# Idle-time matmuls of zeros, new decoding costs and new ranks in a list-scheduled attention and mixer kernel

## The chip, the cores and the metric

The kernel runs on one core of a Trainium2 chip. The metric is the device time of one execution in microseconds (us). Three executions of the kernel before took 624.26, 625.16 and 625.78 us; the median is 625.16 us.

## The reference

For 4 batches of 768 positions, 8 heads of width 64 do attention in which a query sees the 8 global positions and the 96 positions up to and including its own, with a bias that falls with distance. The heads side by side give x (768 x 512 per batch), and two mixers follow:

```
scores = q @ k.T / 8 + bias                       # masked; 8 heads of width 64
x  = softmax(scores) @ v                          # heads side by side: [B, 768, 512]
h  = relu(x.T @ w_tok1) @ w_tok2                  # token mixer, 768 -> 256 -> 768
u  = x + h.T
out = u + relu(u @ w_ch1) @ w_ch2                 # channel mixer, 512 -> 1536 -> 512
```

The mixers' weights arrive as 64-bit floats and are decoded on the chip.

## The kernel before

**Work items.** Nothing is issued in the order of the loops. `run` enters every step into a plan with `add(name, engine, cost, run, after, rank, take, give, form)`: the engine (or a choice of engines, each with its cost), a duration in us, the steps that it comes after, a rank (lower goes first), and the rooms and PSUM banks that it takes and gives back. `Plan.record` walks through time by these durations: whenever an engine is free in the plan, it takes the ready step with the lowest rank for which rooms and banks are free. A step for TensorE whose `form` is another than that of the step before costs 0.1 us more, 0.2 us where one of the two forms is None, and `TURN` times this is added to its rank. Banks are taken from the front of a list of free ones and come back at its end. Then the steps are issued in the order found, and `InOrder` pins it: on the chip each engine runs its steps strictly in the plan's order and waits for their data there. The plan starts VectorE at 1.9, ScalarE at 1.4, GpSimd at 3.6, the queue of transfers at 2.6 us (`BUSY`) and TensorE at 0. Each engine's result is taken to be seen by another after 0.11 to 0.2 us, and a transfer's after 1.5 us (`LATENCY`).

**Attention.** A pair `v` (0 to 47, 12 per batch) is two heads by 256 queries: `load`, `q` (scaled queries), `S` (scores on TensorE, tile sp), `max` (VectorE), `exp` (ScalarE), `sum` and `inv`, `norm` (GpSimd), `T` (transposes, tile tp) and `back`, `V` (tile op), `put` (ScalarE copies op into x). From pair 20 on the transposes are made by transfers (`split`, `turn`, `join`). In the plan a pair's `q` has rank r - 8, its `max` r - 10, `sum` and `inv` r - 12, `T` r - 5, `back` and `V` r - 10, `put` r - 15 and the rest r, with r from `rank("pair", v)`: 10 v in batch 0, `120 + 8.5 i` in batch 1.

**Weights.** Thirty pieces `n` of 128 x 512 go through `load`, `down` (ScalarE, t<-w), `shift` (VectorE TENSOR_SCALAR t<-t), `upper` and `lower` (VectorE SCALAR_TENSOR_TENSOR t<-w,t, both), `high` (ScalarE CAST wc<-t) and `low` (wc<-t,wc, on VectorE or GpSimd). Pieces 0 to 5 are the token mixer's, and from piece 6 on two pieces make one of the 12 slices of the channel mixer's weights. Their rank is `40 + 12 n` below 6 and `100 + 12 n` from 6 on (172 to 448); `high` and `low` go 20 lower.

**Mixers.** Each batch has its tokens (`N`/`xtp`, `J`/`pj`, `U`/`pu`, ranks from -20 in batch 0), and then 24 channel steps k, two passes over the 12 slices: `F` (hp, 12 matmuls), ScalarE's hh, VectorE's hl, and `G` (acc, 12 matmuls over four banks held for a whole pass). `F` of slice f comes after `low` of piece 6 + 2f, `G` after that of 7 + 2f. The rank of batch 0's channel steps is `150 + 5 k`, less 6 for `F` and 30 for hh and hl. At the end of a pass VectorE adds the sums (o<-acc,uh and o<-o,ul) into a tile o, which a transfer stores; the next use of that tile waits for the transfer.

Two matmuls of zeros at the start (`warm`) stand ahead of all.

Of the kernel before, what the change touches and what calls it, by code (L numbers as in the profile page):

```python
# [13 lines left out]
BF16 = mybir.dt.bfloat16  # L14
# [10 lines left out]
P = 128  # L25
# [8 lines left out]
RING = 4  # L34
FAR = 20
NEAR = 2
WARM = 2
PER = H // 2 * NU
PIECES = 6 + 2 * NF
# [6 lines left out]
def f32(ap):  # L46
    return ap.bitcast(F32)
# [40 lines left out]
class Plan:  # L88
# [13 lines left out]
    def add(self, name, engine, cost, run, after=(), rank=0.0, take=(), give=(), form=None):  # L102

        costs = engine if isinstance(engine, dict) else {engine: cost}
        self.work[name] = dict(name=name, costs=costs, run=run, after=sorted(set(after)), rank=rank, take=take, give=give,
                               form=form, choice=isinstance(engine, dict))
# [98 lines left out]
class Fast:  # L207
# [42 lines left out]
    def turn(self, out, in_):  # L250
        self.pe.transpose(out, in_, self.ident)


    def setup(self):

        const, early, dve = self.const, self.early, self.dve
        wp = self.ps.tile([P, 512], F32, tag="b7", name="warm")
        for i in range(WARM):
            self.pe.matmul(out=wp, lhsT=early.warm[:, :P], rhs=early.warm, start=i == 0, stop=i == WARM - 1)
        rel, far, glob = early.rel, early.far, early.glob  # L260
        self.scale(0, dve)
        n = self.soft.tile([P, 4], F32, tag="st", name="n")
        dve.tensor_copy(out=n, in_=early.ni)
        ng, nl = n[:, 0:1], n[:, 2:3]
        nl8 = self.soft.tile([P, 1], F32, tag="st", name="nl8")
        dve.tensor_scalar(out=nl8, in0=nl, scalar1=-8.0, scalar2=None, op0=ALU.mult)

        dve.tensor_scalar(out=glob, in0=glob, scalar1=ng, scalar2=-BIG, op0=ALU.is_ge, op1=ALU.mult)


        self.bo, self.bt, self.be = [const.tile([P, w], F32, tag=t, name=t) for t, w in (("bo", 256), ("bt", P), ("be", 256))]
        bo, be = self.bo, self.be
        dve.tensor_scalar(out=rel, in0=rel, scalar1=nl, scalar2=-BIG, op0=ALU.is_ge, op1=ALU.mult)
        dve.tensor_tensor(out=bo[:, 32:], in0=rel, in1=far, op=ALU.add)
        dve.scalar_tensor_tensor(out=self.bt, in0=glob, scalar=nl8, in1=bo[:, 128:], op0=ALU.add, op1=ALU.max)
        dve.tensor_scalar(out=bo[:, :32], in0=glob[:, :32], scalar1=nl8, scalar2=None, op0=ALU.add)
        for o, i, w in ((0, 32, 128), (160, 160, 96), (128, 0, 32)):
            self.pool.tensor_scalar(out=be[:, o:o + w], in0=bo[:, i:i + w], scalar1=1.0, scalar2=0.0, op0=ALU.mult, op1=ALU.add)


    def weights(self, n):

        add, dve, act = self.plan.add, self.dve, self.act
        g = {}

        def load():  # L290
            x, i = self.pieces[n]
            g["w"] = self.wt.tile([P, 512], I64, tag="w", name="w64")
            self.sp.dma_start(out=g["w"], in_=x[:, i:i + 512])

        def words():
            wi = g["w"].bitcast(I32).rearrange("p (n two) -> p n two", two=2)
            return wi[:, :, 0], wi[:, :, 1]

        def down():
            g["t"] = self.io.tile([P, 512], I32, tag="io", name="t32")  # L300
            act.activation(out=f32(g["t"]), in_=f32(words()[1]), func=AF.Copy, scale=DOWN)

        def shift():
            dve.tensor_scalar(out=g["t"], in0=g["t"], scalar1=3, scalar2=None, op0=ALU.logical_shift_left)

        def upper():
            dve.scalar_tensor_tensor(out=g["t"], in0=words()[1], scalar=-0x80000000, in1=g["t"], op0=ALU.bitwise_and,
                                     op1=ALU.bitwise_or)

        def lower():  # L310
            dve.scalar_tensor_tensor(out=g["t"], in0=words()[0], scalar=29, in1=g["t"], op0=ALU.logical_shift_right,
                                     op1=ALU.bitwise_or)

        def high():
            if n < 6:
                dst, i = (self.W1, self.W2)[n // 3], 512 * (n % 3)
                g["h"], g["l"] = dst[0][:, i:i + 512], dst[1][:, i:i + 512]
            else:
                t = self.wt.tile([P, 1024], F32R, tag="w", name="wc")
                g["h"], g["l"] = t[:, :512], t[:, 512:]  # L320
                (self.A, self.Z)[n % 2][n // 2 - 3] = g["h"], g["l"]
            act.copy(out=g["h"], in_=f32(g["t"]))

        def low(engine):
            engine.tensor_tensor(out=g["l"], in0=f32(g["t"]), in1=f32(g["h"]), op=ALU.subtract)

        r = rank("weights", n)
        add(f"w{n}", "sp", 1.85, load, [f"w{n - 1}"] if n else [], rank("load weights", n), ["w", "raw"])
        add(f"down{n}", "act", 0.6, down, [f"w{n}"], r, ["t"])
        add(f"shift{n}", "dve", 0.45, shift, [f"down{n}"], r)  # L330
        add(f"upper{n}", "dve", 0.75, upper, [f"shift{n}"], r)
        add(f"lower{n}", "dve", 0.85, lower, [f"upper{n}"], r, (), ["w", "raw"])
        add(f"high{n}", "act", 0.52, high, [f"lower{n}"], r - 20, ["w"] if n >= 6 else [])
        add(f"low{n}", dict(dve=0.64, pool=1.35), 0, low, [f"high{n}"], r - 20, (), ["t"])


    def load(self, v):
# [179 lines left out]
    def tokens(self, b):  # L517
# [31 lines left out]
        def high(s):  # L549
            rows[s] = tiles()  # L550
            act.copy(out=rows[s][0], in_=g["tp", s])

        def low(s, engine):
            engine.tensor_tensor(out=rows[s][1], in0=g["tp", s], in1=f32(rows[s][0]), op=ALU.subtract)

        def join(s):
            if s == 0:
                g["pj"] = [self.bank("pj", b, j) for j in range(2)]
            x = rows.pop(s)
            for j in range(2):  # L560
                for n, (w, i) in enumerate(((0, 0), (1, 0), (0, 1))):
                    self.pe.matmul(out=g["pj"][j], lhsT=self.W1[w][:, TOK * s + P * j:TOK * s + P * j + P],
                                   rhs=x[i], start=s == 0 and n == 0, stop=s == NS - 1 and n == 2)
# [35 lines left out]
        for s in range(NS):  # L599
            m, i = divmod(s, 3)  # L600
            if b < NEAR:

# [3 lines left out]
            else:  # L606
                for c in range(4 if i == 0 else 0):
# [5 lines left out]
                    [f"xt{b}{m}{c}" for c in range(4)] + ([f"nl{b}{s - 1}"] if s else []), r[s] - 20, ["p"], ["nat"])  # L613
            add(f"nh{b}{s}", "act", 0.5, lambda s=s: high(s), [f"xw{b}{s}" if b >= NEAR else f"N{b}{s}"], r[s] - 15, [tag, tag])
            add(f"nl{b}{s}", dict(dve=0.62, pool=1.4) if b >= NEAR else dict(dve=0.62), 0, lambda en, s=s: low(s, en),
                [f"nh{b}{s}"], r[s] - 15, (), ["p"] if b >= NEAR else [("xtp", b, s)])
            add(f"J{b}{s}", "pe", 1.39, lambda s=s: join(s), [f"nl{b}{s}", f"low{s // 2}"] + ([f"J{b}{s - 1}"] if s else []),
# [93 lines left out]
    def run(self):  # L711
        self.setup()
        for n in range(PIECES):
            self.weights(n)
        for b in range(B):
            for v in range(PER * b, PER * b + PER):
                self.pair(v)
            self.tokens(b)
            self.channel(b)
        self.plan.record()  # L720


# [13 lines left out]
def rank(kind, *at):  # L736

    if kind == "weights":
        return 40.0 + 12.0 * at[0] if at[0] < 6 else 100 + 12 * at[0]
    if kind == "load weights":  # L740
        n = at[0]
        return 8 + 3 * n if n < 8 else 30 + 4 * n
    if kind == "load":
        return 2.5 * at[0]
    if kind == "pair":
        v = at[0]
        b, i = divmod(v, PER)
        if b == 0:
            return 10.0 * v
        if b == 1:  # L750
            return 120 + 8.5 * i
        return BATCH * b - 60 + 8.5 * i
    if kind == "mix":
        b, k = at
        if b == 0:
            return -20.0 + k
        return (220 + 2 * k if b == 1 else BATCH * b + 10 + 3 * k)
    if kind == "channel":
        b, k = divmod(at[0], 2 * NF)
        return 150 + 5.0 * k if b == 0 else BATCH * b + 100 + 5.5 * k  # L760


BATCH = 140.0


@with_exitstack
# [236 lines left out]
```

## Time and profile before

| what | value |
|---|---|
| median of three executions | 625.16 us |
| the profiled execution's own time | 626.12 us |
| its span, first to last instruction | 624.3 us |
| its mean granted TensorE clock | 0.992 |
| TensorE busy, matmuls | 605.2 us, 97% |
| VectorE busy | 369.5 us, 59% |
| ScalarE busy | 258.3 us, 41% |
| GpSimd busy | 206.2 us, 33% |

The span is from the first to the last instruction of the profiled execution, and 1.8 us of its own time lie around it. That execution took 0.96 us more than the median. Busy shares are averages over stages that have different limits. PE stands for TensorE's matmuls, PEld for its weight loads, DVE for VectorE, ACT for ScalarE, POOL for GpSimd. All steps are issued through one helper, so nearly every row has line 198, and rows are told apart by the names of their tiles.

### The profile page before, as it was taken

Reading aid. Unit: us, or ns where it says so; the run is one execution under the profiler, and the core shown is the slowest. Engines: PE = TensorE matmul, PEld = TensorE weight load, DVE = VectorE, ACT = ScalarE, POOL = GpSimd, SP = SyncE. Lnnn points to the kernel's source line nnn. Section 1 sums busy time; section 2 is a strip of 40 time slices with the busy share of each in tenths; the row PEclk is TensorE's granted clock in tenths of the full one; section 3 lists DMA queues with packets and bytes.
Section 4 is the critical chain, followed back from the end, with each engine's and each line's share of the span. In section 5 each row is a group of like instructions: output and inputs, shape, how many; then the busy total and the mean of one; then the engine's idle time right before and its main releaser. Section 6 shows DMA issues by size and latency. Waiting matters only on the chain. (4 is left out here: it accounts for less than half of the span.)

```text
span 624.3 us, 10468 instructions
## 1 busy us (share of the span) xinstructions
PE 605.2 (97%) x3730; PEld 548.0 (88%) x3730; DVE 369.5 (59%) x949; ACT 258.3 (41%) x711; POOL 206.2 (33%) x314
## 2 busy tenths in 40 slices
PE   5899998999999999999899999999999999999996
PEld 3577896998989999889788999898988999999996
DVE  4999999898733315767686437666755455113112
ACT  5899855753532102655543214444334132110110
POOL 4897755563500101534153024444131115000000
PEclk9999997999999999999999999999999999999999
DMA  7960565242550001477785101578742401001001
GB/s 258 395 225 2 203 239 200 91 148 58 120 110 1 2 0 51 64 184 156 165 163 129 38 1 51 126 145 170 168 80 47 61 1 50 1 1 52 0 1 56
DMA packets 84028, 62.63 MB, mean 100 GB/s; under 512 B 69760, under 2 KB 73984, under 8 KB 83968
## 3 DMA queue, kind: packets, MB, share of 16 engines
q1 hardware_dynamic: 83968, 61.88, 37.7%
q8 instruction: 31, 0.51, 0.3%
q14 instruction: 29, 0.24, 0.1%
HBM read 38.80 MB, written 6.29 MB: 72 GB/s over the span
## 5 line engine op out<-in xcount | busy, mean ns | idle before, releaser
L198 PE MATMUL hp<-uh,wc 128*128 128x384 f32 x768 | 211.5, 337 | 0.2 <-DVE wc L198 0.2
L198 PE MATMUL acc<-hh,wc 128*128 128x384 f32 x768 | 200.6, 342 | 0.0
L198 PEld LDWEIGHTS acc<-hh,wc 128*128 128x128 f32 x768 | 138.4, 190 | 9.3 <-issue 7.2
L198 PEld LDWEIGHTS hp<-uh,wc 128*128 128x128 f32 x768 | 140.7, 189 | 2.7 <-issue 0.9
L198 ACT ACTIVATE hh<-hp 128x384 fp32r<-128x384 f32 x96 | 47.1, 490 | 223.9 <-PE hp L198 203.5
L198 DVE SCALAR_TENSOR_TENSOR hl<-hp,hh 128x384 fp32r<-128x384 f32 x96 | 53.1, 553 | 138.6 <-ACT hh L198 138.3
L198 PE MATMUL acc<-hl,wc 128*128 128x384 f32 x384 | 129.7, 338 | 0.2 <-DVE hl L198 0.2
L198 PE MATMUL hp<-ul,wc 128*128 128x384 f32 x384 | 128.8, 336 | 0.0
L198 POOL TENSOR_SCALAR p<-p,st 128x256 f32<-128x256 f32 (+1 forms) x132 | 85.3, 663 | 58.9 <-DVE st L198 16.1
L198 DVE COPY r<-p 128x1024 uint16<-128x1024 uint16 (+1 forms) x95 | 68.9, 735 | 35.8 <-DMA p<-r 19.5
L198 ACT ACTIVATE p<-p,st 128x256 f32<-128x256 f32 (+1 forms) x132 | 63.7, 485 | 30.0 <-DVE st L198 23.1
L198 PEld LDWEIGHTS acc<-hl,wc 128*128 128x128 f32 x384 | 72.8, 190 | 0.5 <-DVE hl L198 0.5
L198 PEld LDWEIGHTS hp<-ul,wc 128*128 128x128 f32 x384 | 72.5, 189 | 0.0
L198 POOL TENSOR_TENSOR ul<-x,uh 128x384 fp32r<-128x384 f32 x24 | 24.9, 1038 | 133.3 <-ACT uh L198 85.4
L198 DVE SCALAR_TENSOR_TENSOR t<-w,t 128x512 int32<-128x512 int32 x60 | 51.8, 864 | 1.1
L198 POOL TENSOR_SCALAR qs<-e,sc 128x256 f32<-128x256 f32 x36 | 21.0, 585 | 91.4 <-DMA e<-pk 58.8
L198 PE MATMUL sp<-e,qs 64*128 64x256 f32 (+1 forms) x304 | 42.8, 397 | 5.7 <-DVE o L198 1.9
L198 PEld LDWEIGHTS sp<-e,qs 64*128 64x128 f32 x304 | 26.6, 196 | 15.9 <-issue 6.7
L198 POOL TENSOR_SCALAR pp<-pp,st 128x256 f32<-128x256 f32 (+1 forms) x60 | 34.8, 597 | 8.0 <-DVE st L198 5.7
L198 POOL TENSOR_TENSOR wc<-t,wc 128x512 fp32r<-128x512 f32 x16 | 22.6, 1415 | 19.9 <-ACT wc L198 18.6
L198 ACT ACTIVATE pp<-pp,st 128x256 f32<-128x256 f32 (+1 forms) x60 | 28.5, 485 | 1.3 <-DVE st L198 1.3
L198 PE MATMUL op<-r,e 128*64 128x128 f32 (+1 forms) x304 | 28.9, 321 | 0.0
(94 smaller groups left out, 736.6 us busy)
## 6 DMA issues: line engine op xcount, KB each, us to landing
w<-wc SPq DMA_DIRECT2D x24, 512.0 KB, 5.3
e<-pk SPq DMA_DIRECT2D x24, 512.0 KB, 3.8
out<-o SPq DMA_DIRECT2D x32, 192.0 KB, 1.9
e<-pk SPq DMA_DIRECT2D x13, 384.0 KB, 3.6
unit<-pk SPq DMA_DIRECT2D x8, 512.0 KB, 8.5
w<-w SPq DMA_DIRECT2D x6, 512.0 KB, 9.1
p<-r SPq DMA_TRANSPOSE x56, 3.2
unit<-pk SPq DMA_DIRECT2D x2, 384.0 KB, 3.8
```

What stands on the lines that cost most here:

```text
L198: ins = getattr(self.engine, name)(*args, **kw)
```

## The change

A tile of zeros is made after the two warm matmuls, and 100 steps of one matmul each (128 x 128 zeros by 128 x 256 zeros in bf16, into any free bank) are added to the plan after all else, with no predecessors, a cost of 0.11 us, a rank of 1e6 and no form. In the plan's table `upper` and `lower` of pieces 6 to 29 cost 0.85 and 1.3 us in place of 0.75 and 0.85, and their `low` 1.45 in place of 1.35 us on GpSimd. Three ranks are set anew: the weights from piece 6 on (136 to 274 in place of 172 to 448), the pairs of batch 1 (20 higher), the channel steps of batch 0 (10 lower).

```diff
+FILL = 100
...
+    def fill(self, i):
+        self.pe.matmul(out=self.bank("z", i)[:, :256], lhsT=self.zero[:, :P], rhs=self.zero[:, P:], start=True, stop=True)
...
+        self.zero = const.tile([P, P + 256], BF16, tag="zero", name="zero")
+        self.pool.memset(self.zero, 0.0)
...
-        add(f"upper{n}", "dve", 0.75, upper, [f"shift{n}"], r)
-        add(f"lower{n}", "dve", 0.85, lower, [f"upper{n}"], r, (), ["w", "raw"])
+        add(f"upper{n}", "dve", 0.75 if n < 6 else UPPER, upper, [f"shift{n}"], r)
+        add(f"lower{n}", "dve", 0.85 if n < 6 else LOWER, lower, [f"upper{n}"], r, (), ["w", "raw"])
...
-        add(f"low{n}", dict(dve=0.64, pool=1.35), 0, low, [f"high{n}"], r - 20, (), ["t"])
+        add(f"low{n}", dict(dve=0.64, pool=1.35) if n < 6 else LOW, 0, low, [f"high{n}"], r - 20, (), ["t"])
...
+        for i in range(FILL):
+            self.plan.add(f"Z{i}", "pe", 0.11, lambda i=i: self.fill(i), [], 1e6, [("z", i)], [("z", i)])
         self.plan.record()
...
     if kind == "weights":
-        return 40.0 + 12.0 * at[0] if at[0] < 6 else 100 + 12 * at[0]
+        return 40.0 + 12.0 * at[0] if at[0] < 6 else 100 + 6 * at[0]
...
         if b == 1:
-            return 120 + 8.5 * i
+            return 140 + 8.5 * i
...
     if kind == "channel":
         b, k = divmod(at[0], 2 * NF)
-        return 150 + 5.0 * k if b == 0 else BATCH * b + 100 + 5.5 * k
+        return 140 + 5.0 * k if b == 0 else BATCH * b + 100 + 5.5 * k
...
+UPPER, LOWER, LOW = 0.85, 1.3, dict(dve=0.64, pool=1.45)
```

## Rows read from the trace of the kernel before

**Rows 1.** Busy time of each engine in six stretches of the span: us, PE, PEld, DVE, ACT and POOL busy (instructions), granted clock, DMA share, GB/s.

```profile
10.00:20.00 10.00, 9.04 (x55) 5.93 (x56) 6.82 (x35) 7.78 (x30) 6.70 (x16) 1.00 1.01 404
20.00:30.00 10.00, 8.07 (x61) 5.29 (x61) 9.70 (x33) 9.17 (x31) 8.64 (x15) 1.00 1.02 388
30.00:98.00 68.00, 67.37 (x492) 55.35 (x492) 66.83 (x178) 54.81 (x161) 50.23 (x74) 1.00 0.47 168
98.00:110.00 12.00, 9.43 (x41) 7.61 (x38) 10.76 (x29) 6.87 (x20) 7.09 (x9) 0.72 0.62 219
110.00:150.00 40.00, 39.83 (x255) 37.00 (x255) 36.43 (x72) 24.55 (x60) 23.43 (x24) 1.00 0.33 104
150.00:300.00 150.00, 150.00 (x927) 136.95 (x927) 78.97 (x215) 54.76 (x151) 35.88 (x60) 1.00 0.36 79
```

**Rows 2.** The chain that ended last, in order of time (start, us, what): one unbroken run of 24 hp matmuls, which gives their spacing, the end of TensorE's work, and the last piece.

```profile
519.48 4.16 PE hp L198 x24
...
615.16 2.62 PE acc L198 x15
...
619.43 0.56 DVE o L198
```

**Rows 3.** TensorE's matmuls in order of time, 98 to 105 us: start, us, what, count, and in brackets the idle time before it and what ended that. The last row is the busy time of the matmuls with tile wc between 104.40 and 109.05 us, with their count and the granted clock.

```profile
98.19 1.13 PE L198 MATMUL sp<-e,qs 64*128 64x256 f32 x8
100.40 0.67 PE L198 MATMUL sp<-e,qs 64*128 64x256 f32 x2 [1.08 <-issue]
102.56 2.07 PE L198 MATMUL sp<-e,qs 64*128 64x256 f32 x6 [1.49 <-ACT x L198]
104.56 1.01 PE L198 MATMUL acc<-hh,wc 128*128 128x384 f32 x2
...
104.40:109.05 4.65, 4.49 (x14) 0.51 0.52 185
```

**Rows 4.** Some of ScalarE's and VectorE's work in the same stretch, in order of time on each engine, with the same columns.

```profile
98.80 0.62 ACT L198 CAST wc<-t 128x512 fp32r<-128x512 f32 x1 [1.72 <-DVE t L198]
...
102.06 0.44 ACT L198 COPY x<-op 128x128 f32<-128x128 f32 x2
...
99.75 0.55 DVE L198 SCALAR_TENSOR_TENSOR hl<-hp,hh 128x384 fp32r<-128x384 f32 x1
100.21 1.29 DVE L198 SCALAR_TENSOR_TENSOR t<-w,t 128x512 int32<-128x512 int32 x1
```

**Rows 5.** Groups of VectorE's instructions between 82 and 104 us (three of the four kinds that it ran there): operation, tiles, shapes, count, busy us, mean ns of one, idle time before.

```profile
L198 DVE SCALAR_TENSOR_TENSOR t<-w,t 128x512 int32<-128x512 int32 x16 | 16.8, 1049 | 0.4
L198 DVE TENSOR_SCALAR t<-t 128x512 int32<-128x512 int32 x8 | 4.0, 498 | 0.0
L198 DVE SCALAR_TENSOR_TENSOR hl<-hp,hh 128x384 fp32r<-128x384 f32 x4 | 2.2, 552 | 0.0
```

**Rows 6.** All instructions of the decoding tile t on VectorE's two-input operation and of `low` on GpSimd: shortest, median and longest in ns, first and last start in us.

```profile
L198 DVE SCALAR_TENSOR_TENSOR t<-w,t x60: 656/693/1735, 17.3 to 147.4; 128x512 int32<-128x512 int32 x60
L198 POOL TENSOR_TENSOR wc<-t,wc x16: 1270/1415/1714, 69.5 to 140.5; 128x512 fp32r<-128x512 f32 x16
```

**Rows 7.** TensorE's matmuls in the first 22 us, in order of time, columns as in the third group.

```profile
3.86 1.03 PE L198 MATMUL warm<-e 128*128 128x512 bf16 x2 [3.86 <-issue]
4.81 1.65 PE L198 MATMUL sp<-e,qs 64*128 64x128 f32 x8
7.70 1.65 PE L198 MATMUL sp<-e,qs 64*128 64x128 f32 x8 [1.23 <-ACT qs L198]
10.96 1.65 PE L198 MATMUL sp<-unit,qs 64*128 64x128 f32 x8 [1.61 <-DVE qs L198]
12.54 1.54 PE L198 MATMUL tp<-ident,pp 128*128 128x128 f32 x6
...
16.98 0.87 PE L198 MATMUL tp<-ident,pp 128*128 128x128 f32 x6
21.60 1.33 PE L198 MATMUL op<-pp,unit 128*64 128x256 f32 x8 [1.07 <-DVE pp L198]
```

**Rows 8.** The three first waits of VectorE for scores (maxima of pairs 1, 2 and 3), columns as before, and GpSimd's first norms of pair 2.

```profile
9.38 0.29 DVE L198 CUSTOM_DVE_ANT_0 pp<-sp,bt 128x128 f32<-128x128 f32 x1 [1.68 <-PE sp L198]
12.64 0.29 DVE L198 CUSTOM_DVE_ANT_0 pp<-sp,bt 128x128 f32<-128x128 f32 x1 [1.74 <-PE sp L198]
15.70 0.29 DVE L198 CUSTOM_DVE_ANT_0 pp<-sp,bt 128x128 f32<-128x128 f32 x1 [1.32 <-PE sp L198]
17.41 2.47 POOL L198 TENSOR_SCALAR pp<-pp,st 128x128 f32<-128x128 f32 x4 [0.88 <-DVE st L198]
```

**Rows 9.** The second stretch with a lower clock, 305 to 315 us, columns as before: TensorE's rows, then VectorE's row that frees the banks.

```profile
305.72 1.09 PE L198 MATMUL op<-r,e 128*64 128x256 f32 x12
308.35 0.67 PE L198 MATMUL sp<-e,qs 64*128 64x256 f32 x2 [1.54 <-DVE o L198]
...
310.42 1.01 PE L198 MATMUL acc<-hh,wc 128*128 128x384 f32 x2
314.15 0.33 PE L198 MATMUL hp<-uh,wc 128*128 128x384 f32 x1
...
307.69 0.56 DVE L198 TENSOR_TENSOR o<-acc,uh 128x384 f32<-128x384 f32 x1 [4.25 <-DMA out<-o]
```

## The prediction

> **What bounds the kernel now.** I read the busy times by stretch first, then the chain that ended last, then the timeline where TensorE idles or its clock falls. From 110 to 300 us TensorE is busy all the time at the full clock, and the chain behind the last instruction is TensorE's own queue [rows 1, 2]. So the time is TensorE's work, plus what it loses to idling and to a low clock, plus a tail after its last matmul: 615.16 + 2.62 = 617.8, so 6.5 us to the span's 624.3, which no edit touches [rows 2]. A change can win only what is lost now, and pays for every matmul that it adds.
>
> Three stretches lose time.
>
> *The first stall, 98 to 110 us.* Eight score matmuls start at 98.19 and, at the spacing to be seen elsewhere, would be done by 99.3. The next pair's first two start at 100.40 after an idle 1.08, the other six at 102.56 after an idle 1.49, and the sums' matmuls only at 104.56 [rows 3]. The six waited for ScalarE's copy out of the bank (x<-op, 102.06), which stood on ScalarE behind casts that wait for VectorE's decoding [rows 3, 4]. The data for the sums (hl) was done at 100.30 [rows 4]; they merely stood behind the scores. Behind this is VectorE, 66.83 of 68 us busy from 30 to 98 and occupied with decoding from 82 to 104 [rows 1, 5]. After the gaps the clock is low: between 104.40 and 109.05 the granted clock is 0.51, that is mostly the 1.2 GHz level, for 14 matmuls that need 14 x 0.173 = 2.4 us at full clock (0.173 = 4.16/24) [rows 2, 3]. From 99.3 to 109.05 that is 9.75 us; the work in it is 1.06 (eight score matmuls, at the 98.19 row's rate) + 2.4. **Lost: 6.3 us.**
>
> *The second stall, 305 to 314 us.* The matmuls of op end their issue at about 306.7, hp goes on at 314.15. Between lie eight score matmuls and twelve sums: 1.06 + 2.08 = 3.1 of 7.4 us. **Lost: 4.3 us.** The scores wait for VectorE's o, which waited 4.25 us for an earlier store to leave its tile [rows 9].
>
> *The start.* TensorE idles 1.23, 1.61 and 1.07 us at 7, 11 and 21 us, and runs slowly: six transposes take 1.54 us at 12.54 and 0.87 at 16.98 [rows 7].
>
> **The change part by part.**
>
> *The new durations.* The plan held `upper` plus `lower` at 1.60 us a piece. Between 82 and 104 us sixteen of these took 1.049 us on average, 2.10 a piece [rows 5]. So the plan ran up to 0.5 us a piece ahead of the chip, about 4 us over eight pieces, and it put scores and copies on TensorE and ScalarE where it thought VectorE would be through. That is what the queue at 98 to 105 us looks like. With 2.15 the plan is right here. It errs the other way where GpSimd is quiet: the median of one is 693 ns, 1.39 a piece [rows 6]. Too long a duration makes the plan put other work earlier and costs little, since VectorE still starts when its data is there. `low` at 1.45 meets the median of 1.415 [rows 6].
>
> *The new ranks.* Before, the weights (172 on) came after six pairs of batch 1 (120 on); then VectorE had long stretches of decoding alone. A slice costs it 2 x (2.10 + 0.50) + 0.55 = 5.7 us and feeds TensorE 24 x 0.173 = 4.2 [rows 2, 5], so TensorE starves where slices come bare. Now a slice (ranks 136, 142, 148, ...) and 1.4 pairs (140, 148.5, ...) alternate all along; a pair gives TensorE about 3 us (three groups of near 1 us, as the full-clock rows of sp and op) [rows 3, 9]. The pairs that come later fall into 150 to 300 us, where VectorE is busy 79 of 150 us [rows 1]. So I expect the first stall to go. Its price lies between 0 (it only moves) and -6.3; I take **-6.3**, as TensorE's idle time there is the only sizeable one between 30 and 300 us [rows 1]. What is late next is batch 1's tokens, whose pairs now have ranks up to 233; batch 0's channel steps (to 255) still lie behind and cover them.
>
> *The fills at the start.* By the plan's costs S0 runs from 0 to 0.85 and S1 is ready at 1.4 + 0.4 + 0.13 = 1.93, so some 8 fills come between. Pair 2's load ends at 4.0, its scores are ready at 4.0 + 1.5 + 0.3 + 0.11 = 5.9, so some 27 fills stand ahead of S2. A fill's price isn't in the trace; the nearest row is warm: two matmuls of 512 columns take 4.81 - 3.86 = 0.95, so 256 columns take 0.24 us at the low clock [rows 7], and I take half, 0.12, at the full one. On the chip eight slow ones end at about 6.3 + 1.9 = 8.2, so S1 comes 0.5 late. The 27 take 3.2 us at full and 6.5 at low clock; with the clock risen after a few, S2 starts at 13 rather than 10.96. Against that each group of scores, transposes and op up to 17 us shrinks by 0.7. Pair 2's norms start only at 17.41 for another reason, so its delay is covered [rows 8]. VectorE's three waits for scores (1.68, 1.74, 1.32) bound the gain at some 2 us, as half of each is the low clock; the late S2 bounds the loss at 2 us, and at 4.5 if the clock stays low. Both ends are near; I take **0**.
>
> *The other 65 fills.* They fall wherever the plan sees TensorE free. On the chip TensorE has 0.96 + 1.93 us free from 10 to 30 us [rows 1], room for 24. About 40 remain for a stretch in which it is busy 67.37 of 68 us [rows 1]. Each that the chip doesn't wait over costs 0.12: between 0 (they fall where VectorE is late anyway, and hold the clock up) and +4.8. VectorE is as full there as TensorE, so I take half: **+2.4**. The Trainium skill has a rule against this edit: matmuls start and end strictly in program order (TensorE: Matmul & The Clock Gate, What overlaps and what doesn't). By it no fill steps aside for work that is ready, and the sum would hold +4.8 here rather than +2.4. The sums that stood behind six waiting score matmuls at 104.56 agree with it [rows 3, 4].
>
> *The rest.* One memset on GpSimd at the start lies in its idle time before the first norms. The banks of the fills rotate among free ones and have no reader. The second stall comes from a store and its tile in batch 1's end; no edit touches that part, but all before it moves in time: between -4.3 and 0, and I take **0**.
>
> **Sum.** -6.3 + 0 + 2.4 + 0 = -3.9. The profiled execution took 626.1, so 622.2; the median stands 1.0 under it, so **621.2 us**, -0.6%.
>
> **The rivals.**
>
> *Both stalls go and the start gains (A).* For it: a stall that depends on one store's moment seldom outlives a shift of everything before it. Against it: the same ranks from batch 1 on. -6.3 - 4.3 + 1 or 2 of fills: 614 to 617.
>
> *The stall only moves (B).* VectorE is nearly full from 20 to 150 us [rows 1], and no edit takes work from it. If its backlog and not the order starves TensorE, the idle time reappears elsewhere, with a low clock or in fills: -6.3 + 6: 623.9 to 626.4, no change.
>
> *The fills stand in the way (C), slower.* In their place on TensorE they go ahead of work that the plan thought not ready. Their whole length is 100 x 0.12 = 12 us, 35 of them partly at double price (+2 to 4), against some 5 us of idle time in the first 30 us [rows 1, 7]. It decides once more than half of the 12 us fall on work that is ready, and the stall gives back less than 5: +2.5 to +6, 628 to 631. For it: TensorE is full from 30 to 98. Against it: VectorE is too, and a delay up to 4 us there runs into the stall.
>
> *The planner's order is no better.* The new durations are too long outside 82 to 104 us, and the plan may put decoding so early that batch 0's pairs wait. They have ranks under 110 and the weights 136 on, so I count this under B and C.
>
> **How the numbers follow.** Forecast (619 to 623.8) 0.43, A 0.21, B 0.15, C 0.21. About 0.2% (1.25 us) is what a measurement of this kernel can tell from no change. Faster by more: the forecast, A, and a little of B: 0.65; within: 0.13; slower: 0.22. The range runs from 613.5 (A with the start's gain) to 629 (C's middle).
>
> **What would show it.** Right: no idle time of more than 1 us and no clock under 1.0 between 90 and 120 us; TensorE's first transposes of pair 0 take under 1 us; VectorE's decoding and its maxima alternate from 60 to 140 us; some 11 to 14 us of matmuls on the tile zero, most of them before 30 us. Wrong: fills between 30 and 100 us beside ready work, a clock that falls in another place, or hp matmuls that begin later than before. If TensorE idles at all between 150 and 300 us, the delay of batch 1's pairs was mis-sized.

## The result and the profile after

The kernel after takes **630.02 us** (median of five executions, 629.24 to 631.62) beside 625.78 us of the kernel before; the ratio is 1.0073, 95% interval 1.0057 to 1.0088. It is slower, where 621.2 us and a gain were forecast, and 1 us above the end of the range. The profiled execution took 629.54 us with a span of 627.8 us.

First the six stretches of [rows 1] in the profile after (columns as there), then the last link of the chain that ended last, which answers to the acc row of [rows 2].

```profile
10.00:20.00 10.00, 10.00 (x90) 7.27 (x88) 5.98 (x35) 7.61 (x29) 6.21 (x16) 1.00 1.01 406
20.00:30.00 10.00, 9.55 (x81) 6.78 (x78) 9.80 (x29) 8.21 (x27) 9.54 (x14) 1.00 1.02 400
30.00:98.00 68.00, 67.74 (x493) 56.47 (x490) 64.31 (x166) 54.82 (x157) 51.93 (x72) 1.00 0.39 137
98.00:110.00 12.00, 12.00 (x79) 10.35 (x78) 11.83 (x31) 8.15 (x21) 6.88 (x8) 1.00 0.77 292
110.00:150.00 40.00, 35.30 (x243) 27.32 (x241) 37.36 (x101) 31.36 (x90) 29.95 (x39) 1.00 0.61 161
150.00:300.00 150.00, 148.01 (x878) 137.76 (x878) 73.92 (x179) 50.10 (x128) 34.48 (x52) 0.99 0.26 62
```

```profile
618.20 2.61 PE acc L199 x15
```

Read down the PE column against [rows 1]: the stall at 98 to 110 us is gone (12.00 of 12, clock 1.00, where it was 9.43 at 0.72). In its place TensorE is idle for 4.7 of the 40 us from 110 to 150, where it had been idle for 0.17, and for 2 us after 150, where it had not been idle at all. (The clock column says 1.00 from 10 to 20 us in both profiles, though the first six transposes take 1.54 us in one and 0.82 in the other. For the first 20 us the durations tell the pace, not that column.) The last links of the two chains start 618.20 - 615.16 = 3.0 us apart; that is most of the loss.

How much each stretch loses can be counted as the prediction did: its length less the matmuls that start in it, each at its full-clock spacing (hp, acc and pu 0.173 us, sp 0.133, op 0.085, tp and xtp 0.128, pj 0.23; fills count nothing).

| stretch, us | lost before | lost after | difference |
|---|---|---|---|
| 0 to 98 | 15.8 | 17.5 | +1.7 |
| 98 to 110 | 6.6 | 0.3 | -6.3 |
| 110 to 170 | 0.9 | 13.7 | +12.8 |
| 170 to 300 | 2.8 | 1.4 | -1.4 |
| 300 to 320 | 4.5 | 0.4 | -4.1 |
| 320 to 600 | 3.9 | 4.2 | +0.3 |

The sum is +3.0, the distance of the two chains' ends. So both old stalls went, as rival A had it, and one new stall ate more than they gave. Of the 13.7 us lost at 110 to 170, 6.7 are idle time (TensorE is busy 53.31 of the 60 us), about 1 is the eight fills at 110.6 to 112.6, and about 1.5 the low clock told of below. The rest is wider spacing inside rows: eight scores at 127.60 take 1.93 us in place of 1.13. TensorE's timeline shows the gaps; the brackets hold the idle time before a row and what ended it.

```profile
132.76 1.14 PE L199 MATMUL sp<-e,qs 64*128 64x256 f32 x8
...
137.32 0.62 PE L199 MATMUL op<-r,e 128*64 128x256 f32 x2 [1.14 <-DVE r L199]
139.08 1.08 PE L199 MATMUL op<-r,e 128*64 128x256 f32 x10 [1.14 <-ACT r L199]
...
145.76 0.61 PE L199 MATMUL hp<-uh,wc 128*128 128x384 f32 x2 [1.48 <-POOL wc L199]
...
149.58 0.65 PE L199 MATMUL op<-r,e 128*64 128x256 f32 x2 [0.79 <-ACT r L199]
151.57 1.97 PE L199 MATMUL op<-r,e 128*64 128x256 f32 x10 [1.34 <-ACT r L199]
```

Four of these five gaps stand before op<-r, the products of the far pairs (20 and up), whose attention weights (p) are transposed by transfers: VectorE splits them (r<-p), a transfer turns them, ScalarE or VectorE joins them (again r<-p), and only then can TensorE go on. The op row at 151.57 takes 1.97 us for ten matmuls that take 1.08 at 139.08: from 151.5 to 154.5 us the granted clock is 0.50, the 1.2 GHz level, after a stretch (148 to 151) in which TensorE was busy 1.44 of 3 us. (In e13 below, which has the same order, it was busy 0.94 of these 3 us and the clock stayed at 1.00, so no rule can be read from this.) One such pair in the same stretch, the rows of VectorE, of the queue of transfers and of ScalarE:

```profile
130.54 0.97 DVE L199 COPY r<-p 128x1024 uint16<-128x1024 uint16 x1 [0.52 <-POOL p L199]
...
132.11 1.53 DVE L199 COPY r<-p 128x1024 uint16<-128x1024 uint16 x1
131.53 3.38 SPq L199 DMA_TRANSPOSE p<-r  x2
137.33 0.47 ACT L199 ACTIVATE hh<-hp 128x384 fp32r<-128x384 f32 x1
137.70 1.32 ACT L199 COPY r<-p 128x1024 uint16<-128x1024 uint16 x1
```

The second split takes 1.53 us where the plan has 0.68, and ScalarE's join begins at 137.70, behind other work of ScalarE, which is busy without a break from 135.34; it ends at 139.02, and op goes on at 139.08. Before, ScalarE made one such join between 110 and 170 us, after 167; now it makes five, as its group of that stretch shows (columns as in [rows 5]):

```profile
L199 ACT COPY r<-p 128x1024 uint16<-128x1024 uint16 x5 | 6.8, 1351 | 0.6 <-DMA p<-r 0.6
```

Why now? The scores of pairs 20 to 23 in the profile before and in the one after:

```profile
137.13 1.13 PE L198 MATMUL sp<-e,qs 64*128 64x256 f32 x8
...
153.39 3.00 PE L198 MATMUL sp<-e,qs 64*128 64x256 f32 x24
```

```profile
122.36 1.13 PE L199 MATMUL sp<-e,qs 64*128 64x256 f32 x8
...
127.60 1.93 PE L199 MATMUL sp<-e,qs 64*128 64x256 f32 x8
...
132.76 1.14 PE L199 MATMUL sp<-e,qs 64*128 64x256 f32 x8
...
140.09 1.14 PE L199 MATMUL sp<-e,qs 64*128 64x256 f32 x8
```

Decoding's last cast on ScalarE starts at 148.18 us before and at 164.72 after. Before, three of the four pairs came behind the decoding; after, all four come into it, and it ends 16.5 us later.

The first 14 us of TensorE, to be held against [rows 7], and all matmuls on the tile zero (columns as in [rows 6]):

```profile
4.81 1.66 PE L199 MATMUL sp<-e,qs 64*128 64x128 f32 x8
6.40 1.79 PE L199 MATMUL z<-zero 128*128 128x256 bf16 x8
8.12 0.93 PE L199 MATMUL sp<-e,qs 64*128 64x128 f32 x8
8.98 3.12 PE L199 MATMUL z<-zero 128*128 128x256 bf16 x27
12.03 0.93 PE L199 MATMUL sp<-unit,qs 64*128 64x128 f32 x8
...
13.12 0.82 PE L199 MATMUL tp<-ident,pp 128*128 128x128 f32 x6
```

```profile
L199 PE MATMUL z<-zero x100: 269/273/421, 6.4 to 112.6; 128*128 128x256 bf16 x100
```

Eight and 27 fills, S1 at 8.12, S2 at 12.03 and transposes in 0.82 instead of 1.54 us stand nearly where the prediction put them. Of the 100 fills 71 lie before 30 us, 21 between 44 and 71, and 8 at 110.6 to 112.6.

### The profile page after: what moved, and what is told of

It is laid out like the page before. It is cut to its first block, busy times and chain, and to the rows that moved or that the text cites. A ratio compares the mean times of both kernels' runs of the same rounds, so it can differ in the third digit from the quotient of the medians.

```text
span 627.8 us, 10669 instructions
## 1 busy us (share of the span) xinstructions
PE 611.1 (97%) x3830; PEld 551.9 (88%) x3830; DVE 365.7 (58%) x936; ACT 267.5 (43%) x719; POOL 209.8 (33%) x320
## 4 chain that ended last, share of the span: by engine, by line
PE 87%; DVE 4%; POOL 3%; DMA 3%; issue 2%; SPq 0%; ACT 0%; POOLq 0%; DVEq 0%; ACTq 0%
PE acc L199 30%; PE hp L199 30%; PE sp L199 6%; PE op L199 6%; PE pj L199 5%; PE pu L199 5%; DMA e<-pk 3%; PE tp L199 2%; PE z L199 2%; DVE t L199 1%; DVE r L199 1%; PE xtp L199 1%; POOL p L199 1%; POOL wc L199 1%; POOL pp L199 0%
## 5 line engine op out<-in xcount | busy, mean ns | idle before, releaser
L199 POOL TENSOR_SCALAR p<-p,st 128x256 f32<-128x256 f32 (+1 forms) x132 | 78.1, 609 | 67.3 <-DVE st L199 46.1
L199 DVE COPY r<-p 128x1024 uint16<-128x1024 uint16 (+1 forms) x89 | 67.1, 766 | 32.3 <-DMA p<-r 13.8
L199 DVE SCALAR_TENSOR_TENSOR t<-w,t 128x512 int32<-128x512 int32 x60 | 57.5, 958 | 1.2
L199 POOL TENSOR_SCALAR qs<-e,sc 128x256 f32<-128x256 f32 x36 | 22.5, 628 | 76.0 <-DMA e<-pk 41.1
L199 PE MATMUL sp<-e,qs 64*128 64x256 f32 (+1 forms) x304 | 39.6, 383 | 0.1
L199 PE MATMUL op<-r,e 128*64 128x128 f32 (+1 forms) x304 | 31.6, 327 | 4.4 <-ACT r L199 3.3
L199 ACT COPY r<-p 128x1024 uint16<-128x1024 uint16 (+1 forms) x23 | 30.5, 1325 | 12.0 <-DMA p<-r 11.8
L199 PEld LDWEIGHTS op<-r,e 128*64 128x64 f32 x304 | 19.6, 139 | 16.9 <-ACT r L199 4.8
L199 POOL TENSOR_TENSOR wc<-t,wc 128x512 fp32r<-128x512 f32 x20 | 27.1, 1356 | 19.5 <-ACT wc L199 19.5
```

Source lines behind the costliest of these rows:

```text
L199: ins = getattr(self.engine, name)(*args, **kw)
```

## The experiments

Ratios are to the kernel before, run beside each kernel on the same chip; 0.001 is 0.63 us. "Lost" is counted as in the table above, "joins" are ScalarE's r<-p between 110 and 170 us. The plan makes a new order whenever one of its inputs changes, so a part done alone isn't only that part: it is another order, and its trace has to be read.

**Which part.**

*e1, the change without fills.*

```diff
-FILL = 100
+FILL = 0
```

> The kernel after with no fills (FILL = 0). Theory M (the stall moved: the new durations and ranks put TensorE's idle time into 130 to 165 us, about 11 us of loss, and the fills cost little): 626.5 to 628, with TensorE idle for 5 us or more between 130 and 165 us. Rival C (the fills' 12 us stand ahead of ready work and cause the loss): 616 to 620, with no such idle time.

Measured: 623.5 us, ratio 0.9972 (0.9957 to 0.9986). Without fills the rest of the change wins. Neither expectation held: the time lies between the two ranges, and TensorE idles only 1.1 us between 130 and 165.

*e2, the fills alone* (old durations, old ranks).

```diff
-UPPER, LOWER, LOW = 0.85, 1.3, dict(dve=0.64, pool=1.45)
+UPPER, LOWER, LOW = 0.75, 0.85, dict(dve=0.64, pool=1.35)
-            return 140 + 8.5 * i
+            return 120 + 8.5 * i
...
```

> The kernel before with the 100 fills alone; durations and ranks as before. Theory M: 625.8 to 628 (2 us at most for fills beside ready work, the stall at 98 to 110 us still there or partly used up by late TensorE work). Rival C: 629 to 632.

Measured: 625.98 us, ratio 1.0005 (0.9988 to 1.0021): no change in time, as theory M had it. But the stall at 98 to 110 us goes here too (0.6 lost for 6.6), with the old durations and ranks, and 3.7 are lost at 110 to 170.

*e3, the durations alone* (the diff's last line, `FILL = 0`, old ranks).

> The kernel before with the new durations of upper, lower and low alone; no fills, old ranks. If the durations move the stall (VectorE looks fuller to the plan, so joins go to ScalarE and low to GpSimd): 627 to 630, idle time of TensorE behind ScalarE's r and GpSimd's wc between 120 and 170 us. If the ranks do it: 619 to 626, the first stall smaller than before.

Measured: 631.1 us, ratio 1.0084 (1.0066 to 1.0103). The more truthful durations alone cost 0.84%, 1 us more than the higher range. The first stall is gone (lost 0 at 98 to 110), but 13.3 us are lost at 110 to 170, with seven joins.

*e4, the ranks alone* (the three ranks of the diff, `FILL = 0`, old durations).

> The kernel before with the three new ranks alone; no fills, old durations. If the ranks move the stall (the pairs of batch 1 with transposes by transfers meet the last weights): 627 to 630, idle time of TensorE between 120 and 170 us. If the durations do it: 619 to 625.8.

Measured: 624.81 us, ratio 0.9983 (0.997 to 0.9996). Lost 2.6 at 98 to 110 and 5.5 at 110 to 170, one join; the time is in the second range, so the ranks alone don't move the stall.

*e7, fills and ranks; e8, fills and durations* complete the square.

> Fills and new ranks, old durations. If the new durations are what puts TensorE's idle time into 130 to 165 us: 623 to 626.5. If fills and ranks together do it: 628 to 631.

> Fills and new durations, old ranks. If the new durations are what puts TensorE's idle time into 130 to 165 us: 629 to 633, much as with the durations alone (631.1). If the ranks are needed for it: 624 to 627.

Measured: e7 627.91 us, 1.0024 (1.0009 to 1.0039); e8 636.13 us, 1.015 (1.0133 to 1.0167); e7 falls between its two ranges, e8 3 us above both. The ranks win back what the durations cost (e3 against e1: 7 us), and each order loses 3 to 6 us more with fills, except the old one (e2). Each part alone takes most of the first stall away (left of its 6.6 us: 0 with the durations, 2.6 with the ranks, 0.6 with the fills), so no run shows that the old durations were what made it. What the fills do had to be taken apart.

**What the fills cost.**

*e5, all fills planned, none issued.* The order is that of the kernel after.

```diff
-        self.pe.matmul(out=self.bank("z", i)[:, :256], lhsT=self.zero[:, :P], rhs=self.zero[:, P:], start=True, stop=True)
+        return
```

> The kernel after, planned with its 100 fills, none of which is issued: every other step stands in the same order as in after. Theory O (the fills lose time by the order that the plan finds around them, not by their own time on TensorE): 627.5 to 630, TensorE idle for 5 us or more between 130 and 165 us. Rival C (their own time on TensorE is what costs): 617 to 624.

Measured: 627.2 us, ratio 1.0021 (1.0008 to 1.0033), 0.3 us under theory O's range and far from rival C's. The step from e1 to e5 is +0.0049, 3.1 us, with no fill on the chip at all: planned fills push TensorE's other steps about and give another order. That order has the new stall (lost 12.5 at 110 to 170, five joins; e1 5.9 and three).

*e13, the same order, only the 71 fills before 30 us issued.*

```diff
+        if i >= 71:
+            return
```

> The kernel after, in its own order, but only the first 71 of the 100 fills are issued (the ones that ran before 30 us there); the other 29 are planned and left out. Theory E (the early fills lie in idle time and cost nothing, the late ones cost their length and the gaps around them): 627 to 627.7, as without any fill issued (627.2). Rival (the early fills cost, the late ones stand where TensorE idles anyway): 629.5 or more. Between 628 and 629: both pay.

Measured: 627.51 us, ratio 1.0015 (1.0 to 1.0029), that is e5's and in theory E's range. The 71 early fills neither cost nor gain anything that can be told (-0.0006, give or take 0.002 or 1.2 us). By the ratios the other 29 make the rest of the way to 1.0073: 0.0058 or 3.6 us, give or take 1.3, which would be about 0.12 us each, a fill's whole length (27 in 3.12 us). The two profiled executions say less, 627.8 and 626.3 us of span. They run the same order, so their rows can be laid side by side; the kernel after, then e13:

```profile
106.46 2.00 PE L199 MATMUL sp<-e,qs 64*128 64x256 f32 x16
...
117.12 1.13 PE L199 MATMUL sp<-e,qs 64*128 64x256 f32 x8
```

```profile
106.29 2.00 PE L199 MATMUL sp<-e,qs 64*128 64x256 f32 x16
...
116.08 1.21 PE L199 MATMUL sp<-e,qs 64*128 64x256 f32 x8 [0.37 <-POOL qs L199]
```

By 106 us, with 21 of the 29 behind it, the kernel after is 0.17 us late; at 117, with the other eight too, 1.04. So these profiles show the full price for the eight (0.87 us). The 21 took 0.17 us or, if the 0.8 us count that this execution was ahead at 43 us (its scores at 42.92 for 43.72), 1.0, of a length of 2.5. Together that is 1.0 to 1.8 us. Another 0.6 us comes in op rows at 462 to 464 us, where no fill is. Whether this or the ratios' 3.6 holds for the median isn't shown.

*e6 and e9, e1's order with 100 fills put into the gaps that the plan sees* (the plan reckons with none of them). In e6 the fills of a gap go into one bank (`banks[0]`), in e9 round the free ones; the diff is e9's.

```diff
+                if e == "pe" and banks:
+                    for _ in range(min(int((now - free[e]) / 0.11), FILL - fills)):
+                        self.held["z", fills] = banks[fills % len(banks)]
...
```

> The kernel after, planned without fills (the order of e1_no_fill, 623.5), and 100 fills put afterwards into the gaps that the plan leaves on TensorE, without moving anything. Theory O: 622.5 to 625, no more than 1.5 us above e1_no_fill. Rival C: 628 to 632.

> As e6_inserted_fills, but the fills inside a gap go round the banks that are free there instead of all into one. Theory O (fills that move nothing cost little): 623 to 626, each fill 0.11 to 0.22 us after the one before it, and TensorE's clock up before 10 us. Rival C (the fills' own time costs, wherever the order is from): 628 or more.

Measured: e6 657.9 us, 1.0512 (1.0494 to 1.0529); e9 631.85 us, 1.009 (1.0075 to 1.0105). e6 told something else than it was made for: into one bank the fills come 0.42 us apart in its slow first 30 us and 0.32 later, since each waits there for the end of the one before it, and it can't be used for their place. Its rows and then e9's:

```profile
6.39 3.81 PE L206 MATMUL z<-zero 128*128 128x256 bf16 x9
11.89 12.77 PE L206 MATMUL z<-zero 128*128 128x256 bf16 x30
...
28.56 1.51 PE L206 MATMUL tp<-ident,pp 128*128 128x128 f32 x6
...
34.82 0.85 PE L206 MATMUL tp<-ident,pp 128*128 128x128 f32 x6
...
39.19 4.19 PE L206 MATMUL z<-zero 128*128 128x256 bf16 x13
```

```profile
6.41 1.82 PE L206 MATMUL z<-zero 128*128 128x256 bf16 x9
...
10.37 2.78 PE L206 MATMUL z<-zero 128*128 128x256 bf16 x24 [0.29 <-DVE st L206]
```

e9 is 7 us slower than e1 (1.009 against 0.9972): the 100 fills, 12 us long, cost most of their length where the plan has no time for them. That is rival C's range and mechanism, though in the kernel after it has at most 29 fills to work on.

**Where the new stall comes from.** First VectorE, rival B's reason.

*e10, less work for VectorE: `lower` of pieces 6 to 29 isn't issued* (so these weights lack their low words), the order stays that of the kernel after.

```diff
+            if n >= 6:
+                return
```

> The kernel after with the second two-input step of the decoding (lower) left out for the 24 pieces of the channel mixer, so that VectorE has some 25 us less to do between 55 and 165 us; the order is that of after, and the weights lack their low words. Theory S (in the new order the pairs are used up before the decoding is, and TensorE goes at VectorE's pace from 130 to 165 us): 618 to 622, no idle time over 1 us there. Rival J (the waits come from the order alone, through the transfers and ScalarE's joins of pairs 20 to 23): 626 to 630, the waits behind ScalarE's r still there.

Measured: 628.25 us, ratio 1.0029 (1.0016 to 1.0042). VectorE does 8.6 us less between 110 and 170 us (45.43 for 54.07), and 11.1 of the 13.7 us are still lost there, with the same waits behind ScalarE's joins. The time is in rival J's range: VectorE's backlog has a part in it, not the main one.

*e11, pairs 20 to 23 transposed on TensorE; e12 the same with `FILL = 0` and batch 1's pairs at their old rank (120).* The far pairs of batch 1 then have neither split nor join.

```diff
-FAR = 20
+FAR = 24
```

> The kernel after with the transposes of pairs 20 to 23 on TensorE (FAR = 24), as for the pairs before them: no splits, transfers and joins in batch 1. Theory S: their copies load VectorE and ScalarE less, but TensorE takes 4 x 1 us more: 622 to 627, TensorE's idle time at 130 to 165 us under 3 us. Rival D (the decoding alone is what it waits for): 629 or more.

> New durations, new ranks of weights and channel steps, pairs of batch 1 at their old rank, no fills, and pairs 20 to 23 transposed on TensorE. Theory S and O together: 619 to 623, faster than before and than e1_no_fill. If the transposes by transfers were no part of the stall: 625 to 629.

Measured: e11 627.42 us, 1.0032 (1.002 to 1.0045); e12 **621.88 us, 0.9935** (0.9922 to 0.9948), the fastest here, faster than both kernels and in its first range; e11 lies 0.4 us above theory S's. The middle of the stall, 130 to 150 us, in the profiles of the kernel after, of e10 and of e11 (columns as in [rows 1]):

```profile
130.00:150.00 20.00, 15.41 (x101) 11.53 (x99) 19.21 (x48) 14.82 (x39) 15.58 (x20) 1.00 0.78 171
```

```profile
130.00:150.00 20.00, 17.19 (x102) 12.81 (x102) 16.58 (x45) 15.41 (x41) 14.88 (x21) 0.91 0.80 180
```

```profile
130.00:150.00 20.00, 19.48 (x146) 16.45 (x144) 17.35 (x48) 15.73 (x44) 12.88 (x17) 1.00 0.34 116
```

Only e11's TensorE is busy again, with 146 matmuls for 101 (24 of them transposes). Taking the transfers away costs 32 transposes, 32 x 0.128 = 4.1 us of TensorE, and the kernel is 2.6 us faster all the same. It costs more than that: behind TensorE's last matmul the five orders with `FAR = 24` go on for 6.9 to 7.4 us, the same orders with transfers for 5.0 to 5.6; why isn't shown. And `FAR` is an input of the plan too, so each of these runs is another order as well.

*Is it the transfers in other orders too? e14: e1 with `FAR = 24`; e15: e3 with `FAR = 24`; e16: the kernel before with `FAR = 24`.*

> The kernel after with no fills in the plan, and batch 1's pairs 20 to 23 transposed on TensorE in place of by transfers. Theory P (the wait for the far pairs' transfers and ScalarE's joins is lost time in any order): 620.5 to 622.5, under the 623.5 of the same without fills and with the transfers. Rival (that chain is only late in the order that the planned fills made): the four pairs' 32 transposes are 4 us more of TensorE's work, so 625 to 628.

> The kernel before with the new durations alone, and pairs 20 to 23 transposed on TensorE. Theory P (the 5.5 us that the durations alone cost are the same chain of transfers and joins): 624 to 627, against 631.1 with the transfers. Rival (durations cost it elsewhere, by feeding the channel steps too late): 631 to 635, as 4 us of TensorE's work come on top.

> The kernel before, with pairs 20 to 23 transposed on TensorE. Where the chain of transfers isn't late, the edit is 4 us of work without a return. Theory P (the kernel before loses nothing behind these transfers): 627 to 630. Rival (TensorE's work takes the place of idle time here too, as in the first stall): 622 to 626.

Measured: e14 626.59 us, 1.0005 (0.9991 to 1.0018); e15 625.21 us, 0.9984 (0.9969 to 1.0); e16 628.95 us, 1.0046 (1.0031 to 1.0062). For the durations alone it is the transfers: -6.3 us (1.0084 to 0.9984) in spite of the 4.1. In e1 and in the kernel before the edit costs 2 to 3 us: there TensorE waits behind no join between 110 and 170 us, and e14's first expectation is wrong; e15 and e16 came out as their theory P had it.

*e17, the missing corner: no fills, pairs at the old rank, transfers as before.*

> No fills, batch 1's pairs at their old rank of 120, the other new ranks and the new durations, transposes of pairs 20 to 23 by transfers: the fourth corner of the square with 623.5 (pairs at 140, transfers), 626.6 (pairs at 140, TensorE's transposes) and 621.9 (pairs at 120, TensorE's transposes). Theory P (with the new durations and pairs this early, the four pairs' transfers and joins fall beside the decoding, 5 or more joins on ScalarE before 170 us): 627 to 631, idle time of over 5 us at 110 to 170 us. Rival (the old rank of the pairs alone is what made 621.9): 618 to 621, as 4 us of transposes leave TensorE.

Measured: 630.69 us, 1.0073 (1.0049 to 1.0097), in theory P's range. The old rank isn't what made e12 fast: with it, transfers cost 8.6 us net (1.0073 against 0.9935). The stretch 110 to 170 us in the profiles of e17 and e12:

```profile
110.00:170.00 60.00, 53.17 (x314) 43.88 (x313) 50.20 (x119) 39.39 (x95) 33.30 (x39) 0.91 0.54 153
```

```profile
110.00:170.00 60.00, 59.41 (x408) 53.59 (x408) 49.82 (x123) 36.87 (x100) 30.93 (x39) 1.00 0.38 131
```

VectorE and ScalarE are about as busy in both; TensorE runs 314 matmuls in one (16 of them transposes) and 408 in the other (48). Which link TensorE waits behind differs, though. The waits of its queue from 110 to 170 us (us in total, times, longest) in the kernel after and in e17:

```profile
PE op L199 <- ACT r L199: 3.3, 3, 1.3
PE hp L199 <- POOL wc L199: 1.5, 1, 1.5
PE op L199 <- DVE r L199: 1.1, 1, 1.1
```

```profile
PE sp L199 <- POOL qs L199: 2.9, 1, 2.9
PE acc L199 <- ACT wc L199: 2.3, 1, 2.3
```

The orders together (e6 aside); where pairs 20 to 23 are on TensorE, their transposes count as work and not as lost. "Scored early" are how many of the last four pairs of batch 1 start their scores before decoding's last cast:

| order | ratio | lost 98 to 110 | lost 110 to 170 | joins | scored early |
|---|---|---|---|---|---|
| before | 1 | 6.6 | 0.9 | 1 | 1 |
| before, pairs 20 to 23 on TensorE (e16) | 1.0046 | 6.2 | 0.5 | 0 | 1 |
| fills alone (e2) | 1.0005 | 0.6 | 3.7 | 2 | 1 |
| ranks alone (e4) | 0.9983 | 2.6 | 5.5 | 1 | 0 |
| fills and ranks (e7) | 1.0024 | 2.2 | 5.8 | 0 | 0 |
| durations alone (e3) | 1.0084 | 0 | 13.3 | 7 | 4 |
| the same, pairs 20 to 23 on TensorE (e15) | 0.9984 | 0 | 2.5 | 0 | 4 |
| fills and durations (e8) | 1.015 | 0.3 | 15.4 | 6 | 4 |
| ranks and durations (e1) | 0.9972 | 1.3 | 5.9 | 3 | 3 |
| the same, pairs 20 to 23 on TensorE (e14) | 1.0005 | 1.3 | 4.4 | 0 | 2 |
| e1's order, fills in its gaps (e9) | 1.009 | 1.7 | 6.3 | 3 | 3 |
| after's order, no fill issued (e5) | 1.0021 | 0.3 | 12.5 | 5 | 4 |
| after's order, 71 fills issued (e13) | 1.0015 | 0.3 | 12.8 | 5 | 4 |
| after's order, no `lower` issued (e10) | 1.0029 | 0.3 | 11.1 | 5 | 4 |
| after | 1.0073 | 0.3 | 13.7 | 5 | 4 |
| after, pairs 20 to 23 on TensorE (e11) | 1.0032 | 0.3 | 3.9 | 0 | 4 |
| no fills, pairs at 120 (e17) | 1.0073 | 0.1 | 16.0 | 6 | 4 |
| the same, pairs 20 to 23 on TensorE (e12) | 0.9935 | 0.3 | 1.4 | 0 | 4 |

Every order in which all four pairs come before the end of the decoding and go through transfers loses 11 us or more at 110 to 170, and the others lose at most 6.3. The three that bring them as early without transfers (e15, e11, e12) lose 1 to 4.

## Why the prediction was wrong

**The step that failed is the new ranks with the new durations**: "Its price lies between 0 (it only moves) and -6.3", and after it "What is late next is batch 1's tokens [...] cover them". The stall at 98 to 110 us gave back the 6.3 us forecast, and both old stalls went. Late next were not the tokens but batch 1's own far pairs: in the kernel after 12.8 us more are lost at 110 to 170. Without the fills (e1) ranks and durations came to -1.8 us in place of -6.3, with 5.0 us more lost there. That lies inside the bounds, but the bounds were wrong: the durations alone cost +5.3 us (e3), and with all ranks but the pairs' +4.6 (e17). The bound should have been open above 0. I priced the pairs by TensorE's 3 us and not by their path (norm, split, transfer, join), which has three engines and a queue in it.

**The durations**: "Too long a duration makes the plan put other work earlier and costs little". Alone they cost 0.84%. They were right for 82 to 104 us of the kernel before, but durations move with the order: in the kernel after 13 such steps take 1.178 us on average there, 2.36 a piece against the new 2.15. Other steps were never corrected: the split at 132.11 took 1.53 us against 0.68. That these errors are what cost the 0.84% isn't shown.

**The fills at the start**: 0, and 0 it was (e13 against e5). In the same order the first pu matmul comes at 70.06 us with no fill issued (e5) and at 70.38 with the 71 (e13): what the early stages gained in clock didn't reach it. Which engine took it back isn't shown.

**The other fills**: +2.4 for 40 fills at half price. Measured by the ratios: +3.6, give or take 1.3, for 29, that is full price; by the profiles of the same order 1.0 to 1.8 us. So the count was too high, and whether half a price was too low stays open. The Trainium skill (TensorE: Matmul & The Clock Gate, What overlaps and what doesn't) has matmuls start strictly in program order. By it a fill that stands before ready work costs all of itself; the trace agrees for the eight fills at 110.6 us (0.87 us for 8 x 0.12), and the 21 before them don't show it (0.2 to 1.0 us for 21 x 0.12).

**Not in the sum at all**: what planned fills do to the order, +3.1 us (e1 to e5), the other step that failed. The prediction priced only the fills' own time. But in the plan a fill can hold TensorE for up to 0.11 us when a step becomes ready, it takes a bank, and as it has no form the step behind it is planned 0.2 us longer. In e1 one of the four far pairs comes after the decoding (its scores start at 184.6 us), in e5 all four come before it ends. **The second stall**, taken as staying, went: -4.1 us. Rival A put that down to the shift of all before it, but e3 is shifted too and keeps 4.4. What the runs show is that 0.4 to 2.1 us are lost there in every order with the new ranks of the weights and channel steps, and 2.3 to 4.5 in every order with the old; by which path isn't shown.

In ratios: ranks and durations -0.0028, the fills' effect on the order +0.0049, the first 71 fills -0.0006 (within its uncertainty 0), the last 29 +0.0058; together +0.0073, in time -1.8 + 3.1 - 0.4 + 3.6 = +4.6 us.

**The rivals.** B said that the stall moves; it does, and it grew. But its reason, VectorE's backlog, is refuted as the main one by e10. C's time, 628 to 631, is met, and its mechanism explains 1 to 3.6 of the 4.6 us; 3.1 are the fills' too, in a way that C did not name. Of the signs set out beforehand, the clock between 90 and 120 us and the fast first transposes came; "a clock that falls in another place" (151 to 155 us) and TensorE idle after 150 us are the ones that told against the forecast.

**What stays open.** Which link of the far pairs' path matters most. In the kernel after it is ScalarE's join; in e17 TensorE waits behind qs and wc instead, and that qs stands on GpSimd behind four norms that take 3.93 us (134.34 to 138.25). No run took one link away and left the others. Nor is it shown why planned fills bunch the pairs; that is the scheduler's response to a hundred small shifts.

## What to carry to other kernels

In a list-scheduled kernel a stall moves easily: here durations, ranks and fills each took most of it away, alone. Whether time is won depends on the steps that are drawn into the gap: follow the whole path of the work that moves, transfers and joins included, and leave the bound open on the losing side. Work meant for idle time has two prices, its own length wherever the engine isn't really idle, and the change of order that planning it brings; plan it and leave it out to tell them apart. When parts of a change only add up in one order, change one path (here `FAR`) in several orders before calling it the cause.

## What the runs showed of the hardware beyond what was expected

- A full clock can be worth nothing: with the 71 early fills (e13) TensorE's first six transposes took 0.82 us, without them (e5) 1.54, and the kernel reached its first pu matmul at 70.38 and 70.06 us.
- Matmuls of 256 columns that are each a group of their own come further apart when consecutive ones go into the same bank. At the pace of the first microseconds it is 0.42 us (9 in 3.81 us in e6) against 0.22 with the bank changed each time (8 in 1.79 us in the kernel after); at the full clock 0.32 (13 in 4.19) against 0.116 (27 in 3.12, 24 in 2.78). In e6's trace each of them waits for a semaphore that the fill before it raises at its end, so this is the price of that wait, and whether the bank alone would cost anything isn't shown.
- Such spaced matmuls did not bring TensorE to full speed: fill after fill from 11.89 to 24.7 us in e6, the six transposes at 28.56 still take 1.51 us, and only those at 34.82 take 0.85. In the kernel after, with 27 unspaced fills from 8.98 us, those at 13.12 take 0.82.
- VectorE's copies of 128 x 1024 16-bit elements took from 0.68 us (at 149.57) to 1.75 (at 151.00) in one stretch of the kernel after.
